# Seven block products for three column groups of a Fourier mixing layer, with fewer stored sums, on one NeuronCore

## The chip, the cores and the metric

One core of a Trainium2 chip. The metric is the time of one execution in microseconds of the device, lower is better. Engines are called by their short names: PE (TensorE, matmul), PEld (its weight loads), DVE (VectorE), ACT (ScalarE), POOL (GpSimd), SP (SyncE, which here issues most DMAs).

## What is computed

The input x has 2048 rows of 512 numbers. Four layers follow each other, each added to its input after a layer norm of the rows: transform, attention, transform, attention.

```python
x = x + A(layernorm(x)); x = x + B(layernorm(x)); x = x + A(layernorm(x)); x = x + B(layernorm(x))

def A(x):                       # Fourier mixing, real part
    a = x @ dft_hid_re.T; b = x @ dft_hid_im.T
    return dft_seq_re @ a - dft_seq_im @ b

def B(x):                       # 32 heads of 16, four segments of 512 rows
    q, k, v = heads(x @ wq), heads(x @ wk), heads(x @ wv)
    for each segment s:
        p = softmax(q_s k_s^T * scale + mask)       # mask as the reference has it
        o_s = g * (phi(q_s) M / (phi(q_s) z + 1e-6)) + (1 - g) * p v_s
        M += phi(k_s)^T v_s; z += sum(phi(k_s))
    return o @ wo
```

## The kernel before

The transform is taken in the order sequence first, hidden second. For a column group `tcn` of 512 output positions (four of them, `TC`), the kernel forms u = x^T C and x^T S over the 2048 rows, with C and S the 512 columns of the real and imaginary sequence matrix, and then multiplies by the hidden matrices (`hidden`, `hidden_last`). The 2048 rows are 16 tiles of 128; tile k and tile k + 8 (`HALF` is 8) are used together in step k. Each operand is split into a high and a low part in a reduced float32 (`split`: ACT writes the high part, the low part is a subtraction on DVE, or on POOL where asked), and a product is three matmuls, high x high, high x low, low x high (`matmul3`). All matmuls go through one helper, line 82 of the profile; all split copies have line 96, the subtractions line 98, or 94 where DVE does both.

**Transform one** (`direct` is true) works on the plain form. `read_pairs(tcn, k)` loads the four 128x512 blocks of a step (real and imaginary part for tile k and tile k + 8), splits them into the tiles chi and clo (three buffers each), makes four sums of them on DVE, and stores the sums in DRAM (`sums`, 1 MB a step). `contract(tcn)` then makes 8 steps of 2 x 2 x 4 products, 384 matmuls a group, into all eight PSUM banks, and copies the banks out, four on ACT and four on DVE (negated). During column group 0 the rows are also normalised: `normalise` loads two row tiles, makes moments on DVE, the inverse root on POOL, the scaled rows on DVE, the high part on ACT and the low part on POOL, for the tiles xa.

**Transform two** uses seven products for eight, as in fast 2x2 block multiplication: with the rows halved at tile 8 and the columns of x halved at 256, the products P1 to P7 of 256x512 outputs need sums of the blocks of the sequence matrix (those that transform one has stored) and sums of the rows. `read_block` loads one block or stored sum (256 KB) into one of eight places of a ring (`cring`) and splits it. `product` makes P1 and P7 together, then P2 and P4, for all four column groups; each is 8 steps of 2 x 3 matmuls into two banks, 48 in all. `add_rows` loads the rows again, normalises them and makes the row sums xb and xs on DVE. `chained` runs P6, P5, P3 through the same two banks and adds into the results between them. `TERMS` and `CHAIN` tell which result takes which product; results c stay in SBUF.

The order of all work is written by hand: `place(order, generator, slots)` puts each step of a generator into a numbered slot, and slots run in order; a slot in the transforms is about one unit of six matmuls. From that program order a planner with a cost model makes the static order of every engine; `pin` and `keep_in_program_order` hold some instructions to program order, `tc.issue_after` holds one behind another, and `tc.high_priority` moves some forward. `a1`, `b1`, `a2`, `b2` are the first slots of the four layers; transform one has 32 x 8 = 256 slots of products.

**Attention.** For four heads at a time (a unit): `natural_max` makes scores and their row maxima (DVE, line 653), `max_rows` transposes these maxima and puts them by a DMA of ACT's queue into the stacked operand, so that the next scores come out with the maximum subtracted. `softmax_values` makes those transposed scores in ten banks; each is clipped at zero on its diagonal blocks (ACT, line 718), exponentiated (ACT, line 719), masked on POOL (line 722) and multiplied with the values. `output` transposes and scales the result (DVE) and adds the memory part (POOL, line 826). At the very end, `outproj_split` prepares three quarters of each output row tile early, and `transpose_last` the last quarter, which waits for the last unit; then the last matmuls (po), an addition (line 170) and the store.

Of the kernel before, what the change touches and what calls it, by code (L numbers as in the profile page):

```python
# [18 lines left out]
P = 128  # L19
S, D, H = 2048, 512, 32  # L20
DH = D // H
# [20 lines left out]
SOURCE = {"P1": (0, 0), "P2": (0, 1), "P3": (1, 1), "P5": 0, "P7": 1, "P6": 2, "P4": 3}  # L42
# [4 lines left out]
    "P4": (((1, 0), (1, 1), ALU.add),),  # L47
}
CHAIN = {"P6": (1, 0), "P5": (1, 1), "P3": (0, 1)}
PHASES = (  # L50
    (("P1", "P7"), range(4)),
    (("P2", "P4"), range(4)),
)
# [3 lines left out]
def spectral_infini_kernel(  # L57
# [115 lines left out]
    v_tiles = [consts.tile([P, H, VW], F32, name=f"vt{i}") for i in range(6)]  # L173
# [12 lines left out]
    def run_from(t, n, step=1):  # L186
# [3 lines left out]
        (tcn, k): dram.tile([4, P, 512], F32, name=f"sum{tcn}_{k}") for tcn in range(TC) for k in range(HALF)  # L190
# [10 lines left out]
    def place_spectral(x_in, x_out, t0, end, ln_at, direct):  # L201
        xa, xb, xs, us, wdt, c, right = ({} for _ in range(7))
        start = t0
        count = [0]
        ring = []
# [57 lines left out]

        def new_right(src):
            tag = ("chi", "clo")[count[0] % 2]
            count[0] += 1
            t = pair(tag, tag, 3)
            split(t[:, 0], t[:, 1], src)
            return t

        def read_block(tcn, name, k):
            if not ring:
                ring.append(sb.tile([P, 2 * LT, 512], F32, name="cring", tag="xT", bufs=1))
            raw = ring[0][:, blocks_read[0] % (2 * LT)]
            blocks_read[0] += 1
            j = SOURCE[name]
            with tc.issue_after(last_stack[0].ins):
                if isinstance(j, tuple):
                    nc.sync.dma_start(raw, ct[j[0], tcn, k, :, j[1]])
                else:  # L280
                    nc.sync.dma_start(raw, sums[tcn, k][j])
            yield
            right[tcn, name, k] = new_right(raw)
            yield

        blocks_read = [0]

        def read_pairs(tcn, k):
            if not ring:
                ring.append(sb.tile([P, 8, 512], F32, name="sring", tag="xT", bufs=1))  # L290
            if k % 2 == 0:
                raw = [pair("craw", "craw", 2, F32) for _ in range(2)]
            else:
                raw = [ring[0][:, 0:2], ring[0][:, 2:4]]
            halves = [slice(0, 1), slice(1, 2)] if (tcn, k) == (0, 0) else [slice(0, 2)]
            for h in halves:
                for cc in range(2):
                    nc.sync.dma_start(raw[cc][:, h], ct[cc, tcn, k, :, h])
            yield
            for cc in range(2):  # L300
                right[tcn, cc, k] = pair("chi", "chi", 3), pair("clo", "clo", 3)
            for h in halves:
                for cc in range(2):
                    hi, lo = right[tcn, cc, k]
                    with behind_first((tcn, k) == (0, 0)):
                        split(hi[:, h], lo[:, h], raw[cc][:, h])
            yield
            t = ring[0][:, 4:]
            (r0, r1), (i0, i1) = ([raw[cc][:, h] for h in range(2)] for cc in range(2))
            for j, p, q in (0, r0, i0), (1, i0, i1), (2, t[:, 0], i1), (3, t[:, 2], r1):  # L310
                with behind_first((tcn, k) == (0, 0)):
                    summed = pin(V.tensor_tensor(out=t[:, j], in0=p, in1=q, op=ALU.add))
            if (tcn, k) == (1, 0):
                later.append(summed)
            nc.sync.dma_start(sums[tcn, k].rearrange("j p s -> p j s"), t)
            yield
# [5 lines left out]
        def contract(tcn):  # L322
            ps = [[bank(f"u{d}") for d in range(DT)] for _ in range(2)]
            for k in range(HALF):
                for h2 in range(2):
                    for cc in range(2):
                        parts = right[tcn, cc, k]
                        for d in range(DT):
                            matmul3(
                                ps[cc][d],  # L330
                                lambda h: xa[k + HALF * h2][:, h, d * P : (d + 1) * P],
                                lambda h: parts[h][:, h2],
                                (k, h2) == (0, 0),
                                (k, h2) == (HALF - 1, 1),
                            )
# [12 lines left out]

        def product(tcn, name):
            ps = [bank(f"m{m}") for m in range(2)]  # L350
            for k in range(HALF):
                t = right[tcn, name, k]
                for m in range(2):
                    matmul3(
                        ps[m],
                        lambda h: left(name, k, h, m),
                        lambda h: t[:, h],
                        k == 0,
                        k == HALF - 1,
                    )  # L360
                if k < HALF - 1:
                    yield
            for j, base, _ in TERMS[name]:
                if base != j:
                    block(tcn, j)
            for m in range(2):
                for j, base, op in TERMS[name]:
                    dst = c[tcn, j][:, m]
                    if base is None:
                        A.activation(dst, ps[m], AF.Copy)  # L370
                    else:
                        V.tensor_tensor(out=dst, in0=c[tcn, base][:, m], in1=ps[m], op=op)
            yield

        def chained(tcn):
            ps = [bank(f"m{m}") for m in range(2)]
            for name, j in CHAIN.items():
                for k in range(HALF):
                    t = right[tcn, name, k]
                    for m in range(2):  # L380
# [3 lines left out]
                            lambda h: t[:, h],  # L384
# [67 lines left out]
        for n, t in ln_at:  # L452
            place(3, normalise(n), [t, t, t] if n[0] == 0 and direct else [t - 8, t - 3, t])
        if direct:
            for tcn in range(TC):
                t = start + 8 * HALF * tcn
                place(2, contract(tcn), run_from(t, 4 * HALF, 2))
                for k in range(HALF):
                    place(3, read_pairs(tcn, k), [t + 8 * k - 12, t + 8 * k - 4, t + 8 * k + 3])
        else:  # L460
            t = start
            for names, tcns in PHASES:
                for tcn in tcns:
                    for n, name in enumerate(names):
                        at = run_from(t + n, HALF, len(names))
                        place(2, product(tcn, name), at)
                    for k in range(HALF):
                        for n, name in enumerate(names):
                            u = t + k * len(names) + n
                            place(3, read_block(tcn, name, k), [u - 10, u - 4])  # L470
                    t += HALF * len(names)
            u = t
            for tcns in (0, 1), (2, 3):
                at = {tcn: [] for tcn in tcns}
                for name, tcn in itertools.product(CHAIN, tcns):
                    at[tcn] += run_from(t, HALF)
                    for k in range(HALF):
                        place(3, read_block(tcn, name, k), [t + k - 10, t + k - 4])
# [3 lines left out]
            for k in range(HALF):  # L482
                place(3, add_rows(k), [u - 48 + 6 * k, u - 44 + 6 * k])
# [17 lines left out]
    def place_attention(x_in, x_out, t0, w_at, out_at):  # L501
# [195 lines left out]
        def softmax_values(s, g, u):  # L697
# [4 lines left out]
            def scores(dst, *cols):  # L702
# [15 lines left out]
                A.activation(blocks, blocks, AF.Relu)  # L718
# [80 lines left out]
        def output(s, g, u):  # L799
# [15 lines left out]
            for j in range(0, LT, 2):  # L815
# [5 lines left out]
                if s > 0:  # L821
# [4 lines left out]
                    G.tensor_tensor(out=dst, in0=dst, in1=tmp, op=ALU.add)  # L826
# [101 lines left out]
        def transpose_last(s):  # L928
# [9 lines left out]
            split(t[:, 0], t[:, 1], pt)  # L938
# [62 lines left out]
        for n in range(NSEG * USEG):  # L1001
# [3 lines left out]
            place(1.9, max_rows(*unit(n)), [t - 4])  # L1005
            place(1, natural_max(*unit(n)), run_from(t - 17, 10), [t - 7])
            place(0.5, stack(*unit(n)), [t - 21])
        for s in range(NSEG):
# [12 lines left out]
            if s == NSEG - 1 and x_out is out_tiles:  # L1021
                for i in range(LT):
                    place(2, outproj_split(s, i), [o - 12 + i], range(o - 7 + 3 * i, o - 7 + 3 * i + 3), [o + 5 + 1, o + 7])
# [32 lines left out]
    b1 = a1 + TC * 8 * HALF + LEAD  # L1056
# [18 lines left out]
    def setup():  # L1075
        nonlocal ident, ident_b, mask, same_head, gate
        with tc.issue_after(later[0].ins):
# [17 lines left out]
            for v in v_tiles:  # L1095
                G.memset(v[:, :, DH:], 1.0)
# [10 lines left out]
    ident = ident_b = mask = same_head = gate = None  # L1107
    place(5, setup(), [200])
    for t in sorted(slots):
# [45 lines left out]
```

## Time and profile before

| | us |
|---|---|
| median of 3 runs | 1826.85 (1824.24 to 1829.63) |
| the profiled execution | 1832.06 |
| its span, first to last instruction | 1830.3 |
| PE, DVE, ACT, POOL busy | 1776.4, 1300.4, 1053.2, 522.7 |
| products of transform one, first to last start | 7.3 to 362.8 |
| products of transform two, first to last start | 919.0 to 1247.9 |

Groups of instructions are read as: line, engine, operation, output <- inputs with shapes, count, then busy time in us and mean duration of one in ns, then the idle time of the engine just before them and who ended it. A table by stretch gives busy us and, in brackets, the count of instructions begun in the stretch; behind them the granted clock of PE, the busy share of the DMA engines and GB/s. A timeline merges equal neighbours; a bracket behind a line is the idle time before it. Line 98 is every low part, whichever tile it writes; the tile's name tells them apart. Durations of neighbouring instructions of one engine overlap a little, so their sum exceeds its busy time.

### The profile page before, as it was taken

The numbers are of one execution on the slowest core, as the hardware profiler recorded it, in microseconds if no ns is written. First come the engines' busy times: TensorE is split into PE (matmuls) and PEld (weight loads), VectorE is DVE, ScalarE is ACT, GpSimd is POOL, SyncE is SP. The second block draws the span as 40 slices with busy tenths as digits, with TensorE's granted clock in tenths as the row PEclk, the third lists the DMA queues.
The fourth block names the chain that finished last, engine by engine and source line by source line (L and its number), as shares of the span: only waits on it lengthen the run. The fifth ranks groups of instructions, "written<-read, shape, count | busy, mean of one in ns | idle before, by whom it ended". The sixth has DMA issues, their size and how long they took to land. (4 is left out here: it accounts for less than half of the span.)

```text
span 1830.3 us, 31933 instructions
## 1 busy us (share of the span) xinstructions
PE 1776.4 (97%) x10336; PEld 1288.4 (70%) x10336; DVE 1300.4 (71%) x4004; ACT 1053.2 (58%) x2292; POOL 522.7 (29%) x822
## 2 busy tenths in 40 slices
PE   7999999999999999999999999999999999999998
PEld 6788888888656666665568888888875666666654
DVE  7854445574787887877966787667658778787784
ACT  3221222333588787778774555444428787877785
POOL 4400000003344354445531100000134443534442
PEclk9999999999999999999999999999999999999999
DMA  6766665555453443443556777664546334344341
GB/s 220 232 221 197 201 199 185 172 167 169 129 169 123 148 135 99 154 126 126 165 173 198 228 245 220 196 189 133 159 152 186 123 122 152 114 135 141 106 128 42
DMA packets 165656, 296.50 MB, mean 162 GB/s; under 512 B 17776, under 2 KB 66928, under 8 KB 165488
## 3 DMA queue, kind: packets, MB, share of 16 engines
q1 hardware_dynamic: 162224, 293.68, 50.7%
q8 instruction: 81, 1.33, 0.3%
q10 hardware_dynamic: 3264, 0.79, 0.2%
q14 instruction: 87, 0.71, 0.1%
HBM read 192.95 MB, written 100.66 MB: 160 GB/s over the span
## 5 line engine op out<-in xcount | busy, mean ns | idle before, releaser
L653 DVE CUSTOM_DVE_ANT_0 junk<-nat,mask 128x512 bf16<-128x512 f32 (+3 forms) x1024 | 496.6, 485 | 160.7 <-PE nat L82 125.4
L719 ACT ACTIVATE pT<-sT 128x512 f32<-128x512 f32 x640 | 371.5, 598 | 13.1 <-ACT sT L718 0.7
L722 POOL TENSOR_SCALAR_AFFINE_SELECT pT<-pT 128x256 f32<-128x256 f32 (+1 forms) x448 | 197.3, 454 | 476.3 <-ACT pT L719 371.6
L82 PE MATMUL u<-chi,xa 128*128 128x512 f32 x1024 | 317.1, 391 | 7.3 <-DVE xa L94 7.3
L82 PE MATMUL sT<-stkq,stkk 99*128 99x256 bf16 (+3 forms) x1024 | 250.9, 307 | 5.4 <-DMA stkq<-mt 2.1
L82 PE MATMUL nat<-stkk,stkq 96*128 96x512 bf16 (+3 forms) x1024 | 246.7, 302 | 4.5 <-DVE mx L653 2.3
L718 ACT ACTIVATE sT<-sT 128x256 f32<-128x256 f32 (+1 forms) x640 | 208.8, 336 | 50.9 <-PE sT L82 48.2
L82 PEld LDWEIGHTS u<-chi,xa 128*128 128x128 f32 x1024 | 193.2, 189 | 47.1 <-issue 7.3
L145 POOL TENSOR_TENSOR r<-ve,half_neg 128x2 f32<-128x2 f32 (+2 forms) x24 | 19.7, 822 | 657.0 <-DVE ve L143 654.6
L82 PE MATMUL u<-clo,xa 128*128 128x512 f32 x512 | 201.6, 394 | 2.3 <-DVE clo L98 1.9
L82 PE MATMUL y<-wdt,us 128*128 128x512 f32 x768 | 181.9, 390 | 0.0
L82 PEld LDWEIGHTS <-stkk 99*128 99x128 bf16 x1024 | 82.2, 99 | 133.8 <-issue 119.5
L82 PEld LDWEIGHTS y<-wdt,us 128*128 128x128 f32 x768 | 143.6, 188 | 29.7
L82 PE MATMUL pv_bank<-pT,vt 128*17 128x512 f32 (+3 forms) x2048 | 151.6, 436 | 0.0
L82 PEld LDWEIGHTS <-stkq 96*128 96x128 bf16 x1024 | 94.8, 99 | 58.6 <-issue 17.3
L82 PE MATMUL pvv<-wv,xT 128*128 128x512 f32 x384 | 127.3, 443 | 3.6 <-DVE mx L653 3.6
L82 PE MATMUL pqk<-xT,wq 128*128 128x512 f32 x384 | 129.9, 448 | 0.1
L82 PE MATMUL po<-wo,oh 128*128 128x512 f32 x384 | 125.0, 441 | 3.7 <-DVE mx L653 2.2
L82 PE MATMUL pqk<-xT,wk 128*128 128x512 f32 x384 | 123.5, 430 | 0.0
L82 PEld LDWEIGHTS u<-clo,xa 128*128 128x128 f32 x512 | 96.5, 189 | 27.2 <-DVE clo L98 7.4
L82 PEld LDWEIGHTS pv_bank<-pT,vt 128*17 128x17 f32 x2048 | 54.1, 97 | 85.8 <-issue 82.3
L96 ACT ACTIVATE chi<-cring 128x512 fp32r<-128x512 f32 x112 | 70.6, 631 | 64.0 <-DVE clo L98 32.8
(136 smaller groups left out, 3015.9 us busy)
## 6 DMA issues: line engine op xcount, KB each, us to landing
sum<-sring SPq DMA_DIRECT2D x32, 1024.0 KB
cring<-sum SPq DMA_DIRECT2D x128, 256.0 KB
stkq<-scrq SPq DMA_DIRECT2D x64, 384.0 KB
stkk<-scrk SPq DMA_DIRECT2D x64, 384.0 KB
cring<-in_ct SPq DMA_DIRECT2D x96, 256.0 KB
sring<-in_ct SPq DMA_DIRECT2D x32, 512.0 KB
xt<-mid SPq DMA_DIRECT2D x64, 256.0 KB
craw<-in_ct SPq DMA_DIRECT2D x30, 512.0 KB
```

The source lines that it names most:

```text
L82: return tc.keep_in_program_order(op(*args, **kwargs))
L96: pin(A.activation(hi, src, AF.Copy, scale=scale))
L145: G.tensor_tensor(out=r, in0=ve, in1=half_neg[:, :n], op=ALU.pow)
L653: last_max[0] = V.tensor_tensor_reduce(junk[:, :n], src, mask[:, 512 - n :], 1.0, 3e38, ALU.add, ALU.min, dst,)
L718: A.activation(blocks, blocks, AF.Relu)
L719: A.activation(dst, ps, AF.Exp, scale=-SCALE)
L722: G.affine_select(blocks, blocks, pattern=[[0, n] for n in blocks.shape[1:-1]] + [[1, P]], compare_op=ALU.is_ge, fill=0.0, base=0, channel ...
```

## The change

Transform one: column group 0 stays in the plain form (`read_plain`, `contract`), with three of its sums on DVE and one on POOL, made in place in the loaded blocks. When a step's rows have been used, `change_rows` joins the high and low part again on POOL (`whole`), subtracts one half of the columns from the other (POOL) and splits that half anew (`replace`). Column groups 1 to 3 take seven products: P1, P2, P7, P4 step by step together (`read_all`), for the three groups one after the other; then `join_rows` makes the row sums out of the same tiles, on POOL and DVE, and P6, P5, P3 follow together for the three groups (`read_rest`). For these groups one sum is stored with the first pass (index 1), and one with the second (index 0), where four were stored. The loads land in a set of places of two blocks each: four in the ring, two in craw and three in the memory of the value tiles `v_all`, whose ones are set later (`ones`). The stores of sums go through ACT's queue. The sequence matrices lie in DRAM with the four blocks of a step side by side.

Transform two: P1 comes with P7 and P2 with P4 as pairs (`read_pair`); for groups 1 to 3 the second of the pair is made on POOL out of P1's or P2's block and the stored sum. P6, P5, P3 are read for two steps at once (`read_two`).

End of attention two: in the last three units the clips at zero of the odd heads go to DVE; the last unit's memory addition goes from POOL to DVE; the last quarter's split is made in two halves; the last unit's `max_rows` comes a slot earlier; the last row tile's matmuls are placed later.

The diff, cut to its core:

```diff
+    "P6": tuple((j, j, ALU.subtract) for j in ((1, 0), (1, 1), (0, 1))),
+    "P5": tuple((j, j, ALU.add) for j in ((1, 1), (0, 1))),
+    "P3": (((0, 1), (0, 1), ALU.add),),
...
+BLOCK = {"P2": 0, "P1": 1, "P3": 3}
+SUMMED = {"P5": (1, 0), "P7": (2, None), "P6": (3, 1), "P4": (0, None)}
...
+        def whole(i):
+            xn = sb.tile([P, D], F32, name="xn", bufs=2)
+            hi, lo = (xa[i][:, h].bitcast(F32) for h in range(2))
+            G.tensor_tensor(out=xn, in0=hi, in1=lo, op=ALU.add)
+            return xn
+        def replace(i, part, src):
+            split(xa[i][:, 0, part], xa[i][:, 1, part], src, lo_engine=G)
+        def change_rows(k):
+            xn = whole(k)
+            G.tensor_tensor(out=xn[:, b], in0=xn[:, a], in1=xn[:, b], op=ALU.subtract)
+            replace(k, b, xn[:, b])
+        def join_rows(k):
+            e, o = whole(k), whole(k + HALF)
+            V.tensor_tensor(out=e[:, b], in0=e[:, b], in1=o[:, b], op=ALU.add)
+            V.tensor_tensor(out=e[:, a], in0=e[:, b], in1=e[:, a], op=ALU.subtract)
+            V.tensor_tensor(out=o[:, a], in0=e[:, b], in1=o[:, a], op=ALU.subtract)
+            replace(k, a, e[:, b]); replace(k, b, e[:, a]); replace(k + HALF, a, o[:, a])
...
+        def read_plain(tcn, k):     # loads and splits as before, then, in place:
+                pin(V.tensor_tensor(out=re[:, 1], in0=re[:, 1], in1=im[:, 0], op=ALU.add))
+                pin(G.tensor_tensor(out=im[:, 0], in0=im[:, 0], in1=im[:, 1], op=ALU.add))
+                pin(V.tensor_tensor(out=im[:, 1], in0=re[:, 1], in1=im[:, 1], op=ALU.add))
+                pin(V.tensor_tensor(out=re[:, 0], in0=re[:, 0], in1=im[:, 1], op=ALU.add))
+            nc.scalar.dma_start(sums[tcn, k][:, :2], re)
+            nc.scalar.dma_start(sums[tcn, k][:, 2:], im)
+        def read_all(tcn, k):
+            fetch(re, ct[tcn, k, :, :2]); fetch(im, ct[tcn, k, :, 2:])
+            pin(G.tensor_tensor(out=im[:, 0], in0=im[:, 0], in1=im[:, 1], op=ALU.add))
+            later.append(pin(V.tensor_tensor(out=im[:, 1], in0=re[:, 1], in1=im[:, 0], op=ALU.add)))
+            right[tcn, "P2", k], right[tcn, "P1", k] = rights(re)
+            pin(V.tensor_tensor(out=re[:, 0], in0=re[:, 0], in1=im[:, 1], op=ALU.add))
+            split(hi[:, 0], lo[:, 0], im[:, 0]); split(hi[:, 1], lo[:, 1], re[:, 0])
+            nc.scalar.dma_start(sums[tcn, k][:, 1], im[:, 1])
+        def read_rest(tcn, k):      # two steps; x: P5 and P6 of one step, y: P3 of both
+                    pin(V.tensor_tensor(out=x[h][:, 0], in0=x[h][:, 1], in1=y[:, h], op=ALU.subtract))
+            right[tcn, "P5", k], right[tcn, "P6", k] = rights(x[0])
+            right[tcn, "P3", k], right[tcn, "P3", k + 1] = rights(y)
+            right[tcn, "P5", k + 1], right[tcn, "P6", k + 1] = rights(x[1])
+                    nc.scalar.dma_start(sums[tcn, k + h][:, 0], x[h][:, 0])
+        def read_pair(tcn, k, names):
+            fetch(two[:, 0], ct[tcn, k, :, BLOCK[names[0]]])
+            fetch(two[:, 1], summed(tcn, k, names[1] if tcn == 0 else "P6"))
+            if tcn:
+                op = ALU.subtract if names[1] == "P7" else ALU.add
+                pin(G.tensor_tensor(out=two[:, 1], in0=two[:, 1], in1=two[:, 0], op=op))
...
         if direct:
+            place(2, contract(0), run_from(t, 4 * HALF, 2))
+                place(3, read_plain(0, k), [t + 8 * k + d for d in (-12, -4, 1, 4)])
+                place(3, change_rows(k), [t + 8 * k + 9])
+            t += 8 * HALF
+            for tcn in range(1, TC):
+                for n, name in enumerate(names):            # P1, P2, P7, P4
+                    place(2, product(tcn, name), run_from(t + n, HALF, 4))
+                    place(3, read_all(tcn, k), [t + 4 * k + d for d in (-14, -7, -4, -2, 0)])
+                t += 4 * HALF
+                place(3, join_rows(k), [t + 6 * k - 28])
+            for tcn in range(1, TC):
+                for n, name in enumerate(CHAIN):            # P6, P5, P3
+                    place(2, product(tcn, name), run_from(t + n, HALF, 3))
+                    place(3, read_rest(tcn, k), [t + 3 * k + d for d in (-12, -6, -3, 0)])
+                t += 3 * HALF
...
-                A.activation(blocks, blocks, AF.Relu)
+                if x_out is out_tiles and (s * NG + g) * NU + u >= NSEG * USEG - 3 and cols[0][0] % 2:
+                    V.tensor_scalar_max(blocks, blocks, 0.0)
+                else:
+                    A.activation(blocks, blocks, AF.Relu)
...
-                    G.tensor_tensor(out=dst, in0=dst, in1=tmp, op=ALU.add)
+                    (V if last else G).tensor_tensor(out=dst, in0=dst, in1=tmp, op=ALU.add)
...
-            split(t[:, 0], t[:, 1], pt)
+            for half in slice(0, 2 * P), slice(2 * P, 4 * P):
+                split(t[:, 0, half], t[:, 1, half], pt[:, half])
...
-    b1 = a1 + TC * 8 * HALF + LEAD
+    b1 = a1 + (8 + 7 * (TC - 1)) * HALF + LEAD
```

More of the change, by code (lines that the diff above doesn't have):

```diff
@@ L203, in place_spectral @@
         start = t0
-        count = [0]
-        ring = []
+        homes, released, clock, singles = [], {}, [0], [0]
         def normalise(n):
@@ L262, in left, with raw_pair @@
             return src[:, h, (col + m) * P : (col + m + 1) * P]
-        def new_right(src):
-            tag = ("chi", "clo")[count[0] % 2]
-            count[0] += 1
+        def raw_pair(own=False):
+            clock[0] += 1
+            if not homes:
+                ring = sb.tile([P, 2 * LT, 512], F32, name="cring", tag="xT", bufs=1)
+                homes.extend(ring[:, j : j + 2] for j in range(0, 2 * LT, 2))
+                if direct:
+                    homes.extend(pair("craw", "craw", 2, F32) for _ in range(2))
+                    homes.extend(spare[:, j : j + 2] for j in range(0, 6, 2))
+            elif not direct and len(homes) == LT and clock[0] > 24:
+                homes.extend(pair("craw", "craw", 2, F32) for _ in range(2))
+            j = min((j for j in range(LT if own else len(homes)) if released.get(j, 0) is not None), key=lambda j: released.get(j, 0))
+            released[j] = None
+            return homes[j], j
@@ L286, in place_spectral @@
[L286 to L298, printed above, removed]
-            yield
[L300 to L306, printed above, removed]
-            yield
[L308 to L315, printed above, removed]
```

183 lines of the change are left out of this document (133 added, 50 removed).

## The prediction

> **What bounds the kernel now.** I read the page first, then the busy time of each engine by stretch, then who waits for whom on TensorE, then the groups by shape inside chosen stretches, and last the timelines of VectorE and GpSimd where both are busy.
>
> ```profile
> span 1830.3 us, 31933 instructions
> PE 1776.4 (97%) x10336; PEld 1288.4 (70%) x10336; DVE 1300.4 (71%) x4004; ACT 1053.2 (58%) x2292; POOL 522.7 (29%) x822
> ...
> L82 PE MATMUL u<-chi,xa 128*128 128x512 f32 x1024 | 317.1, 391 | 7.3 <-DVE xa L94 7.3
> L82 PE MATMUL u<-clo,xa 128*128 128x512 f32 x512 | 201.6, 394 | 2.3 <-DVE clo L98 1.9
> ```
>
> TensorE is busy for 97% of the span, and transform one is 1024 + 512 = 1536 of its matmuls. The mean of 391 ns is not what one costs, because matmuls overlap in the pipe; the cost is the spacing, and the table by stretch has it (busy us and count of each engine, then granted clock, DMA share, GB/s):
>
> ```profile
> core 0: us, PE busy (x) PEld busy (x) DVE busy (x) ACT busy (x) POOL busy (x), PEclk, DMA share, GB/s
> 31.40:42.76 11.36, 11.28 (x50) 8.85 (x49) 10.24 (x18) 2.97 (x5) 5.59 (x4) 1.00 0.74 233
> 186.00:272.00 86.00, 86.00 (x381) 71.19 (x381) 40.90 (x52) 18.41 (x19) 0.00 (x0) 1.00 0.59 193
> 965.00:1030.00 65.00, 64.76 (x293) 53.23 (x292) 44.99 (x79) 29.13 (x51) 11.77 (x10) 1.00 0.63 200
> 1054.00:1118.00 64.00, 64.00 (x284) 53.01 (x283) 57.42 (x110) 35.88 (x64) 0.00 (x0) 1.00 0.79 252
> ```
>
> In the second row (inside the third column group of transform one) 86.0 us hold 381 or 382 matmuls, 0.225 us each, with VectorE only 48% busy and GpSimd empty. So this stage is bound by TensorE alone, and a matmul less is 0.225 us less as long as that stays so. The last row is transform two, already in the seven-product form: 284 matmuls in 64 us, the same 0.225, although VectorE is at 90%. The first row is one of the eight steps of column group 0. A step is 48 matmuls, 10.8 us of TensorE, but it takes 11.36 us; the timeline of GpSimd shows the period, and VectorE is busy for 10.24 of it:
>
> ```profile
> 30.42 4.90 POOL L98 TENSOR_TENSOR xa<-xn,xa 128x512 fp32r<-128x512 f32 x2 [2.12 <-ACT xa L96]
> 38.96 0.69 POOL L145 TENSOR_TENSOR r<-ve,half_neg 128x2 f32<-128x2 f32 x1 [3.65 <-DVE ve L143]
> 41.78 4.90 POOL L98 TENSOR_TENSOR xa<-xn,xa 128x512 fp32r<-128x512 f32 x2 [2.12 <-ACT xa L96]
> ```
>
> So column group 0 is bound by VectorE, not by TensorE. Why VectorE needs 10.24 us shows when its groups from 20 to 95 us (first three rows, GpSimd active) are set against the same groups from 120 to 340 us (last three, GpSimd empty):
>
> ```profile
> L98 DVE TENSOR_TENSOR clo<-sring,chi 128x1024 fp32r<-128x1024 f32 x8 | 13.5, 1685 | 0.4 <-ACT chi L96 0.2
> L312 DVE TENSOR_TENSOR sring<-sring 128x512 f32<-128x512 f32 x12 | 11.0, 957 | 0.0
> L312 DVE TENSOR_TENSOR sring<-sring,craw 128x512 f32<-128x512 f32 x8 | 9.8, 1229 | 0.0
> ...
> L312 DVE TENSOR_TENSOR sring<-sring 128x512 f32<-128x512 f32 x41 | 26.4, 685 | 2.9 <-DMA sum<-sring 2.9
> L98 DVE TENSOR_TENSOR clo<-sring,chi 128x1024 fp32r<-128x1024 f32 x20 | 24.5, 1223 | 53.3 <-ACT chi L96 53.3
> L312 DVE TENSOR_TENSOR sring<-sring,craw 128x512 f32<-128x512 f32 x20 | 13.7, 685 | 0.1
> ```
>
> The same subtraction takes 1685 instead of 1223 ns, the sums 957 and 1229 instead of 685. Per step that is 2 x 0.46 for the subtractions and about 4 x 0.29 for the sums (a mean over the two rows and the six sums that stayed at 0.69), 2.1 us beside two GpSimd subtractions. So one GpSimd 128x512 operation costs VectorE about 1.05 us here. What it takes GpSimd itself undisturbed, and what a narrow one takes, are in these two rows (timeline, then chain of waits):
>
> ```profile
> 448.62 1.17 POOL L593 TENSOR_TENSOR parts<-rem,parts 128x512 bf16<-128x512 f32 x1 [0.74 <-ACT parts L589]
> ...
> 1821.15 0.46 POOL onat L826
> ```
>
> 1.17 us for 512 columns, 0.46 for 128; I take 0.70 for 256, between them. In transform two the price is smaller. Groups from 965 to 1030 us, with three GpSimd pairs, and from 1054 to 1118 us, with none:
>
> ```profile
> L98 DVE TENSOR_TENSOR clo<-cring,clo 128x512 fp32r<-128x512 f32 x19 | 15.0, 792 | 5.1 <-ACT clo L96 5.1
> L98 DVE TENSOR_TENSOR chi<-cring,chi 128x512 fp32r<-128x512 f32 x19 | 14.5, 763 | 6.5 <-ACT chi L96 5.8 <-DMA xt<-mid 0.7
> L166 DVE TENSOR_SCALAR xn<-xt,row_mv,row_r 128x512 f32<-128x512 f32 x8 | 5.3, 699 | 0.1
> ...
> L98 DVE TENSOR_TENSOR clo<-cring,clo 128x512 fp32r<-128x512 f32 x24 | 16.5, 687 | 2.3 <-ACT clo L96 2.1
> L372 DVE TENSOR_TENSOR c<-c,m 128x512 f32<-128x512 f32 x11 | 7.3, 681 | 0.6 <-PE m L82 0.6
> L166 DVE TENSOR_SCALAR xn<-xt,row_mv,row_r 128x512 f32<-128x512 f32 x14 | 7.2, 542 | 0.0
> L241 DVE TENSOR_TENSOR xn<-xn 128x256 f32<-128x256 f32 x7 | 2.9, 419 | 0.0
> ```
>
> The excess is 19 x 0.105 + 19 x 0.076 + 8 x 0.157 = 4.7 us for six GpSimd operations, 0.78 each. The c<-c,m rows read PSUM, and two that ran beside a GpSimd pair kept their time:
>
> ```profile
> 1009.19 1.37 DVE L372 TENSOR_TENSOR c<-c,m 128x512 f32<-128x512 f32 x2 [1.76 <-PE m L82]
> ...
> 1009.63 3.00 POOL L98 TENSOR_TENSOR xa<-xn,xa 128x512 fp32r<-128x512 f32 x2 [4.19 <-ACT xa L96]
> ```
>
> So p, the loss of VectorE for one more GpSimd 128x512 operation, lies between 0 (beside idle time or such evictions) and 1.05 us. By width, a 256-column operation counts 0.6 p. The whole forecast hangs on p.
>
> The Trainium skill, page "SBUF — State Buffer", section "Who interferes with whom", says that a VectorE instruction with two SBUF inputs contends with a GpSimd instruction that reads SBUF, and that the one that comes second is blocked for the whole instruction of the other. The trace agrees with 1685 against 1223 ns, and with the unchanged PSUM evictions. By that rule alone, each new operation in a saturated queue would cost its 1.17 us, about the upper end; that is the second rival below.
>
> **The change part by part** (plus is slower).
>
> *Matmuls.* Column groups 1 to 3 go from 384 to 7 x 8 x 2 x 3 = 336 matmuls each: 3 x 48 x 0.225 = **-32.4 us**. Transform two keeps its 1344.
>
> *Column group 0 (bound by VectorE, 11.36 us a step).* VectorE loses one sum (-0.685). GpSimd gets one sum (1), the joining of the two halves (1), a 256-column subtraction and a 256-column remainder (0.6 each), 3.2 p a step. Ends: at p = 0 the step falls to TensorE's 10.8, -0.56; at 1.05 it is +2.68. Over seven steps -4 to +19. At p = 0.5 it is +0.92 a step: **+6**.
>
> *Products P1, P2, P7, P4 of groups 1 to 3.* A step is 24 matmuls, 5.4 us. VectorE: one subtraction of 1.22, two of 0.685, two sums of 0.685, and 6 evictions in 8 steps, together 4.47 us by durations. Durations overlap: in the stretch 1054:1118 the nine groups sum to 65.2 us and the engine was busy 57.42, so I scale by 0.88 to 3.93. With one GpSimd sum it is 3.93 + p, under 5.4 for every p: **0**. Three buffers of each of chi and clo leave four of the step's six-matmul units, 5.4 us, to refill one, against 1.22 us of VectorE and 1.06 of ScalarE:
>
> ```profile
> L96 ACT ACTIVATE chi<-sring 128x1024 fp32r<-128x1024 f32 x32 | 33.5, 1059 | 103.9 <-PE u L82 84.0 <-DVE sring L312 14.9 <-DMA sring<-in_ct 4.9
> ```
>
> DMA: 1 MB in and 0.25 MB out in 5.4 us is 243 GB/s, and the row 1054:1118 ran at 252 with TensorE unbroken: 0.
>
> *Joining the rows, eight times, in the 49 six-matmul units (66 us) before the last is needed.* GpSimd: two 128x512 and three 128x256, 3.8 p. VectorE: three of 0.42, scaled 1.1. All eight: 8 x (1.1 + 3.8 p). Room: 37.8 us at (3.93 + p)/5.4, then 28 us of the last three products, where two steps (8.1 us) need three subtractions of 1.22, two of 0.685 and three evictions, scaled 6.25 (77%). At p = 0.5: 24 us to place, 6.8 + 6.4 us of room: **+11**. Ends: 0 at p = 0; 40.8 - 9.4 = +31 at 1.05. What is queued behind a late remainder is the first use of these rows as P6, P5 and P3, that is TensorE itself.
>
> *Handing over banks.* After P6, P5 and P3 of a group VectorE makes 12 evictions, 8.2 us by 0.681, while TensorE finds two spare banks and reaches P6's banks after 4.05 us. Ends 0 and 3 x 4.2 = +12.5; it has the two other products to run through, so I stay near the low end: **+2**.
>
> *Queues.* The sums' writes move from SP to ScalarE's queue, 16 + 24 + 24 issues. The nearest row is a 0.73 us issue during which ScalarE went on working:
>
> ```profile
> 1800.74 0.58 ACT L719 ACTIVATE pT<-sT 128x512 f32<-128x512 f32 x1
> 1800.99 0.73 ACTq L692 DMA_DIRECT2D stkq<-mt  x1
> 1801.22 0.27 ACT L718 ACTIVATE sT<-sT 128x128 f32<-128x128 f32 x1
> ```
>
> Even if each blocked it, a step of 5.4 us would have about 2 x 1.06 + 0.73 of ScalarE: 0. SP no longer holds loads behind a store, but TensorE lost nothing to loads: 0. The ones in the value tiles are set later, 0.9 us of GpSimd beside other work: 0.
>
> *Transform two.* 48 GpSimd additions between load and split. In 1054:1118 (23.7 steps of 12 matmuls) VectorE has 6.6 us free and needs 23.7 p more: +5 at p = 0.5, 0 to +18 over its ends. In 965:1030 it is 45.0 + 24 p in 65 us: 0 (to +5). **+5**.
>
> *End of attention two.* The waits of TensorE, the chain of waits, and the clips' group from 1797 us on:
>
> ```profile
> PE sT L82 <- ACT pT L719: 1.5, 1, 1.5
> PE oT L82 <- POOL onat L826: 0.8, 1, 0.8
> PE po L82 <- ACT oh L96: 0.7, 1, 0.7
> ...
> 1821.15 0.46 POOL onat L826
> 1821.65 0.86 PE oT L82 x4
> 1822.54 0.60 ACT oh L96
> ...
> L718 ACT ACTIVATE sT<-sT 128x256 f32<-128x256 f32 (+1 forms) x18 | 5.6, 327 | 0.0
> ```
>
> Four of ten clips at zero per unit leave ScalarE (0.33 us each), which takes most of the 1.5 us stall; VectorE's addition in place of 0.46 saves some 0.2, half a copy before the first use 0.25. Ends -4 (all three waits and a little more) and +1 (clips queue behind maxima): **-2**.
>
> *Sum:* -32.4 + 6 + 0 + 11 + 2 + 0 + 5 - 2 = -10.4 us. The profiled execution took 1832.06 us (span 1830.3), so it would take 1821.7; it stands 5.2 us above the median of the runs, so the median goes from 1826.85 to **1816.5**. 0.3% (5.5 us) is about what a measurement of this kernel can tell from no change.
>
> **The rivals.**
>
> *Covered (p up to 0.25).* The planner puts the new GpSimd work beside evictions and waits. For it: VectorE at 48% before. Against: the joins leave no such place. At 0.25: -32.4 + 1 + 1.5 + 2 + 0 - 2 = -30, 1797.
>
> *Blocked (p about 0.78, transform two's own price).* VectorE and GpSimd take turns, and VectorE becomes the bound of transform one. -32.4 + 7 x 1.81 + (32.5 - 11.3) + 3 + 12 - 2 = +14.5, **1841**, slower. For it: both measured prices, 0.78 and 1.05. Against: those were pairs right behind a full VectorE queue. It decides from p = 0.62, where the sum is zero; at 1.05 it is over +40.
>
> *The matmuls go, the time does not: bank turn-around.* With p = 0.5 and the handover at its upper end of 12.5 us, the sum is 0, 1827. For it: the four interleaved products fill all eight banks. Against: each product ends six matmuls after the one before it, which staggers the evictions.
>
> **How the numbers follow.** Forecast (p from 0.35 to 0.55, 1804 to 1821) 0.33, covered 0.19, blocked 0.33, turn-around 0.15. Faster 0.33 + 0.19 = 0.52, same 0.15, slower 0.33. I take p = 0.5 because one end is measured where everything was queued and the other is what idle time gives; the new work meets both. Between 0.25 and 0.35, and above 0.55, the cases meet. The range runs from p about 0.25 to about 0.85: 1797 to 1846, with about 1 in 10 left out on either side; the likeliest case's own is 1804 to 1821.
>
> **What would show it.** Transform one has 1392 matmuls; in its groups 1 to 3 a count near 222 in 50 us with short gaps means covered, VectorE above 95% busy with subtractions above 1.4 us means blocked. A step of group 0 should last 12.3 us. A break should stand where the joins run, just after group 3's P4, and little at the handovers. In transform two the stretch with the row sums should lose about 5 us. I am wrong if TensorE waits on DMA in the new products, or if the shared memory of value tiles and loads delays the start of attention one.

## The result and the profile after

The change made the kernel slower: a median of 1857.08 us (1855.27 to 1859.52) against 1826.89, a ratio of 1.0163 with a 95% interval of 1.0151 to 1.0176. The forecast was 1816.5, with a range of 1797 to 1846; the rival "blocked" had 1841 and the right sign. In later comparisons the kernel before stood at 1831 to 1833 us, so each version below is compared with the runs of before beside it: the changed kernel is "30.2 above". Single runs of the kernel before went from 1827 to 1836 us there, so a version that ran once is read by its trace.

The page of the changed kernel, then the first and last starts of the hidden products (y) and of the first products with row sums in transform two (xb):

```profile
span 1857.8 us, 32230 instructions
PE 1761.4 (95%) x10192; PEld 1261.1 (68%) x10192; DVE 1455.6 (78%) x4113; ACT 1100.1 (59%) x2367; POOL 726.5 (39%) x964
...
L82 PE MATMUL y<-wdt,us x768: 387/389/501, 375.7 to 1387.2; 128*128 128x512 f32 x192
L82 PE MATMUL m<-chi,xb x192: 389/389/389, 1150.8 to 1258.0; 128*128 128x512 f32 x192
```

The 144 matmuls are gone (10336 to 10192), VectorE is busy 155 us longer and GpSimd 204. Set side by side, by first starts in the two traces:

| stretch of the traces | before | after | difference |
|---|---|---|---|
| first product to the 384th (column group 0) | 7.3 to 101.7 | 7.3 to 111.6 | +10 |
| from there to the first y | 261.4 | 264.1 | +2.7, with 32.4 us of matmuls less |
| first y to the first product of transform two | 555.9 | 556.7 | +1 |
| from there to the first xb product | 199.9 | 218.4 | +18.5 |
| from there to the last y | 236.5 | 236.4 | 0 |
| from there to the end | 474.9 | 470.6 | -4 |

So groups 1 to 3 of transform one gave back 35 us where 32.4 were won, and transform two lost 18.5 without a matmul changed. GpSimd's timeline in column group 0, one step long:

```profile
33.16 3.16 POOL L98 TENSOR_TENSOR xa<-xn,xa 128x512 fp32r<-128x512 f32 x2 [1.94 <-ACT xa L96]
36.28 2.27 POOL L256 TENSOR_TENSOR xn<-xa 128x512 f32<-128x512 f32 x1
38.64 1.60 POOL L265 TENSOR_TENSOR xn<-xn 128x256 f32<-128x256 f32 x1
40.77 0.73 POOL L98 TENSOR_TENSOR xa<-xn,xa 128x256 fp32r<-128x256 f32 x1 [0.53 <-ACT xa L96]
41.60 1.07 POOL L145 TENSOR_TENSOR r<-ve,half_neg 128x2 f32<-128x2 f32 x1
42.64 1.29 POOL L362 TENSOR_TENSOR craw<-craw 128x512 f32<-128x512 f32 x1
45.88 3.15 POOL L98 TENSOR_TENSOR xa<-xn,xa 128x512 fp32r<-128x512 f32 x2 [1.94 <-ACT xa L96]
```

The step is 12.7 us where it was 11.36. The joining addition (line 256) takes 2.27 us, the sum of the same size (line 362) 1.29. In the same step on VectorE:

```profile
35.10 4.54 DVE L98 TENSOR_TENSOR clo<-craw,chi 128x1024 fp32r<-128x1024 f32 x2
42.71 1.24 DVE L150 TENSOR_TENSOR rt<-r 128x2 f32<-128x2 f32 x1 [0.59 <-POOL r L145]
```

The two wide subtractions and the joining addition lie over each other from 36.28 us on. Line 150 begins 0.07 us behind GpSimd's sum and ends with it, at 43.95 against 43.93 us. VectorE's groups in that part (20 to 107 us), then between 230 and 300 us, where the rows are joined, then in transform two from 1086 to 1150 us:

```profile
L98 DVE TENSOR_TENSOR clo<-cring,chi 128x1024 fp32r<-128x1024 f32 x6 | 13.7, 2300 | 0.0
L150 DVE TENSOR_TENSOR rt<-r 128x2 f32<-128x2 f32 x6 | 7.4, 1239 | 3.6 <-POOL r L145 3.6
...
L98 DVE TENSOR_TENSOR clo<-cring,chi 128x1024 fp32r<-128x1024 f32 x8 | 13.2, 1660 | 0.0
...
L166 DVE TENSOR_SCALAR xn<-xt,row_mv,row_r 128x512 f32<-128x512 f32 x14 | 13.1, 962 | 0.0
```

The wide subtraction takes 2300 ns, against 1685 before and 1223 alone; the row scaling 962 against 542. Line 150 works on two numbers a partition and takes 1.24 us; before it took 0.16:

```profile
L150 DVE TENSOR_TENSOR rt<-r 128x2 f32<-128x2 f32 x7 | 1.1, 162 | 6.1 <-POOL r L145 6.1
```

The table by stretch, transform one where the rows are joined, then transform two:

```profile
200.00:250.00 50.00, 45.83 (x194) 35.38 (x192) 47.15 (x49) 20.43 (x33) 31.19 (x21) 1.00 0.53 173
250.00:300.00 50.00, 41.55 (x165) 31.02 (x164) 46.12 (x50) 21.54 (x33) 31.87 (x24) 0.97 0.45 155
...
1000.00:1050.00 50.00, 46.84 (x195) 36.68 (x193) 38.38 (x54) 19.38 (x34) 29.01 (x20) 0.97 0.62 202
1050.00:1100.00 50.00, 49.64 (x218) 40.77 (x219) 44.63 (x59) 25.64 (x44) 21.15 (x14) 1.00 0.68 220
1100.00:1150.00 50.00, 45.39 (x188) 35.77 (x187) 49.93 (x81) 23.91 (x44) 18.29 (x10) 0.97 0.67 217
```

222 matmuls would be a full stretch. VectorE is at 92 to 100% in the rows that lose most but one: from 1000 to 1050 us it is at 77%, and 27 matmuls are missing all the same. The granted clock of 0.97 in three of the rows is a stretch of 3.4 us at half clock in each: matmuls stand 0.43 us apart in it, 8 in place of 15, so it can cost 1.6 us. Transform two has three such stretches (before, its products had none), but they do not make its loss: a version below, without the early row changes, has one there and takes 219.0 us, not less than 218.4. In the row from 1000 to 1050 us GpSimd's queue had just stood still for 12.9 us, with additions behind a remainder that waited for ScalarE:

```profile
986.02 1.28 POOL L422 TENSOR_TENSOR cring<-cring 128x512 f32<-128x512 f32 x1
1000.22 3.00 POOL L98 TENSOR_TENSOR xa<-xn,xa 128x512 fp32r<-128x512 f32 x2 [12.93 <-ACT xa L96]
1003.18 2.99 POOL L422 TENSOR_TENSOR craw<-craw 128x512 f32<-128x512 f32 x2
```

That gave two theories. "Port": GpSimd and VectorE take turns and lengthen each other's instructions. "Queue": the new work stands behind operations that wait, in an engine that executes in order.

### The profile page after: what moved, and what is told of

It is laid out like the page before. It is cut to its first block, busy times and chain, and to the rows that moved or that the text cites. A ratio compares the mean times of both kernels' runs of the same rounds, so it can differ in the third digit from the quotient of the medians.

```text
span 1857.8 us, 32230 instructions
## 1 busy us (share of the span) xinstructions
PE 1761.4 (95%) x10192; PEld 1261.1 (68%) x10192; DVE 1455.6 (78%) x4113; ACT 1100.1 (59%) x2367; POOL 726.5 (39%) x964
## 3 DMA queue, kind: packets, MB, share of 16 engines
q8 instruction: 80, 1.31, 0.3%
## 4 chain that ended last, share of the span: by engine, by line
PE 66%; DVE 17%; issue 6%; POOL 5%; DMA 3%; ACT 2%; SPq 0%; DVEq 0%; ACTq 0%; POOLq 0%
PE m L82 16%; PE pqk L82 9%; PE y L82 8%; PE pv_bank L82 7%; PE sT L82 7%; PE nat L82 6%; PE pvv L82 4%; PE po L82 3%; DVE junk L787 3%; DVE clo L98 3%; POOL xa L98 2%; DVE c L495 2%; PE on L82 1%; PE pm L82 1%; DVE xn L166 1%
## 5 line engine op out<-in xcount | busy, mean ns | idle before, releaser
L82 PE MATMUL m<-chi,xa 128*128 128x512 f32 x1056 | 316.9, 400 | 11.1 <-ACT chi L96 3.1
L82 PE MATMUL m<-clo,xa 128*128 128x512 f32 x720 | 238.0, 401 | 18.6 <-DVE clo L98 18.4
L82 PEld LDWEIGHTS m<-chi,xa 128*128 128x128 f32 x1056 | 201.7, 192 | 58.9 <-DVE c L495 4.3
L82 PEld LDWEIGHTS m<-clo,xa 128*128 128x128 f32 x720 | 135.9, 190 | 59.4 <-DVE clo L98 32.5
L96 ACT ACTIVATE chi<-cring 128x512 fp32r<-128x512 f32 (+1 forms) x137 | 99.5, 730 | 110.3 <-PE m L82 46.7
L82 PE MATMUL pv_bank<-pT,v_all 128*17 128x128 f32 (+3 forms) x2048 | 153.7, 436 | 1.3 <-POOL pT L859 1.3
L82 PEld LDWEIGHTS pv_bank<-pT,v_all 128*17 128x17 f32 x2048 | 53.6, 97 | 89.5 <-issue 84.3
```

Of the source, the lines that this page charges most:

```text
L82: return tc.keep_in_program_order(op(*args, **kwargs))
L96: pin(A.activation(hi, src, AF.Copy, scale=scale))
```

## The experiments

**All new work on VectorE.** The additions, remainders and differences that the change gave to GpSimd run on VectorE.

```diff
-                pin(G.tensor_tensor(out=two[:, 1], in0=two[:, 1], in1=two[:, 0], op=op))
+                pin(V.tensor_tensor(out=two[:, 1], in0=two[:, 1], in1=two[:, 0], op=op))
...
-            split(xa[i][:, 0, part], xa[i][:, 1, part], src, lo_engine=G)
+            split(xa[i][:, 0, part], xa[i][:, 1, part], src)
```

> All additions and remainders that the change gave to GpSimd run on VectorE. Theory 'port': a GpSimd operation costs a busy VectorE about what its own would (0.6 to 1.05 us against 0.6), so little moves: 1842 to 1857 us, a step of column group 0 stays at 12.7 us (11.36 + 0.61 + 2 x 0.36 for the three operations). Theory 'queue': GpSimd executes in order, and its work for the matmuls stands behind operations that wait (12.9 us at 987 us, 10.7 at 205); then the losses of transform two (18.5 us) and of the joins mostly go: 1825 to 1838, with group 0 unchanged.

Measured: 1826.64 us against 1832.82, ratio 0.9967 (0.9955 to 0.9978). The number lies in the range of "queue", but that range was set from 1826.9 us for the kernel before, so it meant 2 us faster to 11 slower, and 6 faster lies outside it. The wording of "queue" fails too: the step of group 0 fell from 12.7 to 11.6 us, which it had as unchanged. The first y starts at 347.1 (375.7 with GpSimd), and transform two takes 207.2 us (218.4). In the step only the old GpSimd remainders are left; the joining addition still meets them:

```profile
34.50 1.76 DVE L256 TENSOR_TENSOR xn<-xa 128x512 f32<-128x512 f32 x1 [1.19 <-POOL xa L98]
...
L98 DVE TENSOR_TENSOR clo<-cring,chi 128x1024 fp32r<-128x1024 f32 x6 | 7.3, 1217 | 0.0
```

The subtractions are back at 1217 ns. "A GpSimd operation costs VectorE what its own would" was too cheap: taking over the work made VectorE's other work shorter. It is busy 1426.0 us here, with all of the new work, and 1455.6 in the changed kernel, where GpSimd does part of it. The version is 6 us below before where the changed kernel is 30 above.

**The kernel before, with the rows' low parts on VectorE.**

```diff
-                engines = ... else {"lo_engine": G, "hi_engine": A}
+                engines = ... else {"lo_engine": V if direct else G, "hi_engine": A}
```

> The kernel before, with the low parts of the normalised rows of transform one on VectorE in place of GpSimd. Port: the two subtractions cost VectorE 2.1 us a step on GpSimd and 1.2 on its own queue, so the step falls from 11.36 to TensorE's 10.8: 3 to 4 us faster, 1823. Rival (offloading does relieve VectorE): its step grows by 1.2 us, 8 us slower, 1835.

Measured: 1833.10 against 1832.82, ratio 1.0 (0.9987 to 1.0012). Both expectations miss. From 20 to 100 us, first this kernel, then the kernel before:

```profile
20.00:100.00 80.00, 77.69 (x338) 62.95 (x337) 65.80 (x127) 24.61 (x32) 4.18 (x6) 1.00 0.71 230
...
20.00:100.00 80.00, 79.57 (x340) 62.44 (x339) 70.14 (x111) 23.47 (x31) 37.53 (x20) 1.00 0.71 229
```

VectorE was relieved by 4.3 us, as "port" says, and TensorE made no more matmuls (338 and 340). So column group 0 of the kernel before was not held by VectorE's load. What holds its step at 11.36 us instead of 10.8 stays open.

**Transform two: GpSimd writes a constant instead of adding.** Same place in the queue, same wait for the load of the block that is written, nothing read (the sums for P7 and P4 of groups 1 to 3 are left out). **And: subtractions of the same size, on memory that nothing waits for.** They wait for no load either.

```diff
-                pin(G.tensor_tensor(out=two[:, 1], in0=two[:, 1], in1=two[:, 0], op=op))
+                pin(G.memset(two[:, 1], 0.001))
...
+                v5 = v_tiles[5][:, :, :DH]
+                pin(G.tensor_tensor(out=v5, in0=v5, in1=v5, op=ALU.subtract))
```

> The 48 additions of transform two are replaced by a GpSimd write of a constant into the same block, at the same place in its queue and with the same waits (left out: the sums for P7 and P4 of three column groups). It reads nothing. Port: all 18.5 us of transform two come back, about 1838. Queue: the first stretch (970 to 1056 us, some 10 us) stays lost, only the stretch with the row sums (some 8) comes back: 1847 to 1850.

> The 48 additions are replaced by GpSimd subtractions of the same size on memory that nothing waits for (left out: the same sums). They read, but no split waits for them. Port: the loss stays, 1852 to 1857. Queue: the first stretch comes back (10 us), the row sums' stretch stays: 1845 to 1849.

Measured: 1844.14 us and 1854.13, 11 and 21 above before. Transform two to its first xb product took 201.6 us with writes and 210.6 with the operations apart, against 199.9 before and 218.4 in the changed kernel. First the writes, then the operations apart:

```profile
1000.00:1050.00 50.00, 48.78 (x216) 40.04 (x215) 35.50 (x65) 23.55 (x41) 12.17 (x17) 1.00 0.71 223
1050.00:1100.00 50.00, 50.00 (x222) 41.40 (x221) 38.88 (x69) 26.26 (x46) 9.10 (x17) 1.00 0.75 231
...
L422 POOL MEMSET cring<- 128x512 f32 x34 | 18.1, 536 | 45.7 <-DMA cring<-sum 45.7
...
1000.00:1050.00 50.00, 46.50 (x195) 36.98 (x194) 38.37 (x53) 19.51 (x34) 27.45 (x23) 0.97 0.64 196
1050.00:1100.00 50.00, 46.86 (x199) 35.74 (x199) 49.30 (x62) 24.47 (x43) 26.32 (x20) 1.00 0.67 213
```

With writes, 17 of the 18.5 us are back, though they stand in the same queue behind the same remainders (longest wait there 14.3 us). "Queue" had the first stretch as lost; it is not, so a waiting queue head alone does not cost this time. With reading operations that nobody waits for, 10.7 us stay lost and 7.8 come back. "Port" had all of it staying and "queue" about 8 us, with the first stretch restored, which it is not (195 matmuls). So contention by itself is the larger part, and the rest appears when the splits also wait for the slowed additions. Each of the two ran once, but this stretch repeats: the changed kernel and the next two versions, which leave it as it is, took 218.4 to 219.0 us. One difference stays: a write takes 0.54 us and an addition 1.3 to 1.7, so the chain was shorter too. With the additions done on VectorE (the first experiment) the stretch took 207.2 us. The Trainium skill, page "SBUF — State Buffer", section "Who interferes with whom", has VectorE's two-input instructions contend with GpSimd's reads and not with its writes; 201.6 against 218.4 us agrees.

**Transform one without the early row changes, and without the joins.** The two `place` lines of `change_rows` and of `join_rows` are taken out, one in each kernel.

> The changed kernel without change_rows (left out: the subtraction of one half of the columns from the other in the eight early row tiles, so P7, P5 and P6 read the plain rows). Port: the GpSimd operations of a step fall from 6 to 3 and the step of column group 0 from 12.7 to about 11.2 us, so group 0 ends near 100 us in place of 111; all else stays: about 11 us less than the changed kernel, 1846. Rival (group 0 is held by the moved sum and the in-place order): it stays near 111, 1857.

> The changed kernel without join_rows (left out: the row sums for P6, P5 and P3). Port and queue both: the matmuls missing between 232 and 300 us come back, some 18 us, 1839. Rival (the bank handovers of P6, P5 and P3 lose the time): no more than 5 us come back, 1852.

Measured: 1855.85 and 1838.64 us, 24 and 7 above before (the changed kernel is 30 above). Without the changes the step is 11.56 us and the 384th matmul starts at 104.5, nearer to the 100 of "port" than to its rival's 111, although line 150 still takes 1.24 us. The first y comes 10.8 us earlier, at 364.9, of which 3.7 are left at the end of the trace; the rest is lost in stretches that this version does not touch, 2.9 between the first y and transform two and 3.7 behind the last y. Without the joins the first y comes at 351.4, 24.3 earlier:

```profile
250.00:300.00 50.00, 48.09 (x211) 39.01 (x210) 37.46 (x46) 17.76 (x17) 0.00 (x0) 1.00 0.57 189
```

211 matmuls where the changed kernel has 165. The joins are the larger part, and the bank handovers alone are not what was lost. But this version leaves out the joins' work on VectorE and ScalarE too, so the 24.3 us are not GpSimd's alone.

**The kernel before with the new end alone.**

> The kernel before with nothing but the new end of attention two. From the two traces: the distance from the last row-maximum matmul's stage to the end is 4.3 us shorter, so 4 us faster than before. The prediction's own term: 2 us.

Measured: 1831.98 against 1831.47, ratio 1.0 (0.999 to 1.0009). The end brings nothing that the runs can tell (the interval is about 1.8 us either way); in the traces the time from the last row-maximum matmul to the end fell from 33.0 to 32.1 us. The 4 us that the changed kernel seemed to win behind its last y are not from this edit: the stretch from the last y to the last row-maximum matmul, which no kernel here edits but for its last units, takes 441.9 us before, 438.5 changed, 442.0 here.

**All on VectorE, and the low parts too.** To the all-VectorE version come the low parts of transform one's rows on VectorE and an earlier start of transform two's row sums.

```diff
...
-                place(3, add_rows(k), [t - 48 + 6 * k, t - 44 + 6 * k])
+                place(3, add_rows(k), [t - 76 + min(12 * k, 28 + 6 * k), t - 72 + min(12 * k, 28 + 6 * k)])
```

> The version with all new work on VectorE, and further the low parts of transform one's rows on VectorE (no GpSimd reads left in column group 0) and the row sums of transform two begun earlier, at unequal distances from slot 56 on. Port: the step of group 0 goes from 11.6 to about 11, 4 us; transform two loses 2 to 4 us in place of 7: 8 us faster than the all-VectorE version, 0.8% faster than before. Rival (VectorE's own load is the bound now): no gain over the all-VectorE version, 0.3% faster than before.

Measured: 1821.92 against 1831.47, ratio 0.9947 (0.9932 to 0.9962). The first y starts at 343.6, 3.5 us earlier than in the all-VectorE version; transform two still takes 206.7 us where 3 to 5 us less were expected, and the gap moved to 1002 to 1018 us. The gain over before, 0.5%, lies between the two expectations (0.8 and 0.3%).

**That version with one kind of work back on GpSimd.** First the 32 sums, then the joining and changing of rows.

> The best version with only the sums of transform one (8 + 24) back on GpSimd; the joining of rows stays on VectorE. In the best version the hidden products of layer one start at 343.6 us, in the changed kernel at 375.7. Port: VectorE loses about what it is spared, so they start at 342 to 347. Queue (sums stuck behind joining work that waits): nothing waits in front of the sums here, so likewise 342 to 346; the two theories part on the next run.

> The best version with only the joining and splitting of rows (change_rows, join_rows) on GpSimd, the sums on VectorE. Port: the loss adds up, so most of the 32 us is here, hidden products start at 362 to 372 us, and the wide subtractions of VectorE in column group 0 take over 1.7 us. Queue: the loss needs both kinds on one queue; here at most 12 us, 346 to 356.

Measured: 1836.88 and 1829.21 us, against 1831.5 before. The first y starts at 356.9 and 352.1, 13.3 and 8.5 later than in the version without GpSimd. Both theories miss on the sums (342 to 347 expected); on the joins "port" misses (362 to 372) and "queue" is right (346 to 356). Together they are 21.8 us of the 32.1 between that version and the changed kernel; the rest needs both, or the low parts (3.5). Half of the sums' price has its place in group 0: its 384th matmul starts at 108.2 in place of 101.3, with VectorE's wide subtraction undisturbed and line 150 not:

```profile
L98 DVE TENSOR_TENSOR clo<-cring,chi 128x1024 fp32r<-128x1024 f32 x6 | 7.3, 1221 | 0.0
...
L150 DVE TENSOR_TENSOR rt<-r 128x2 f32<-128x2 f32 x6 | 7.4, 1238 | 5.3 <-POOL r L145 5.3
```

One GpSimd sum a step falls on the first of the small operations between the moments and the scaled rows, and adds 1.08 us to the chain that the next step's rows wait for; the step is 12.0 us. In the version without that sum line 150 takes 154 ns. The other 6.4 us are lost behind group 0, and where is not shown. With the joining and changing of rows on GpSimd the 384th matmul starts at 100.5: alone, the row changes cost nothing in group 0, while taking them out of the changed kernel brought 7.1 us there. So the losses do not add.

**The row sums ten slots later.** `t - 66 + min(10 * k, 18 + 6 * k)` for the first of the two slots.

> The best version with the row sums of transform two begun 10 slots later and evenly spaced, so that they do not meet the last normalised rows (1002 to 1018 us, some 4 us of matmuls missing there). If that meeting makes the gap: 2 to 4 us faster than the best version, 0.7% faster than before. If ScalarE's wait for the normalised rows makes it (5.4 us idle at 1001 us): no change, 0.5% faster.

Measured: 1819.48 against 1831.52, ratio 0.9934 (0.9913 to 0.9954), the best of all; its interval overlaps that of the version before it. Transform two takes 203.9 us to its first xb product, 2.8 less, which is what the first reading gave (2 to 4). From 1000 to 1050 us 15 matmuls are still missing, so ScalarE's wait remains a candidate for the rest:

```profile
1000.00:1050.00 50.00, 47.33 (x207) 38.31 (x206) 44.52 (x84) 26.16 (x46) 3.66 (x3) 1.00 0.72 234
```

## Why the prediction was wrong

- *Matmuls, -32.4 us:* right. 144 are gone at 0.225 us each, and in the best version, with the work and the low parts on VectorE, 19.9 us of it arrive (first y at 343.2 against 363.1).
- *Column group 0, +6:* measured +10. Worked back, a step of +1.34 us is p = 0.63, not 0.5. The reading that VectorE's load holds this part was wrong (relieving it by 4.3 us changed nothing); in the changed kernel the wide subtractions took 2.30 us and the operation of 0.16 us became 1.24. Neither is the whole of it: without the row changes the 1.24 stay and the step is 11.56. With the row changes on GpSimd and nothing else of it, group 0 loses nothing either. What makes the step 12.7 us when they come together is not separated.
- *Joins +11 and handover +2:* measured 35. This is the term that was mis-sized most: leaving the joins out brings 24.3 us back, and leaving the new work and the low parts off GpSimd in all of transform one, group 0 with it, 32.1. With all of it on VectorE the stretch behind group 0 still takes 242.3 us, 13 more than 261.4 less 32.4: as much as the two terms gave. So about 22 of the 35 us go with the engine.
- *Products P1, P2, P7, P4, 0:* nearly so where the joins do not run: 216 of 222 matmuls from 150 to 200 us.
- *Transform two, +5:* measured +18.5. Only the stretch with the row sums was given a loss; the stretch before it, priced at 0 by VectorE's average load, lost as much. An average over 65 us does not see a wait between a load, an addition and a split.
- *End, -2:* -0.9 in the traces, nothing that the runs can tell.
- *Queues and DMA, 0:* not contradicted; without GpSimd 220 of 222 matmuls ran from 150 to 200 us in the first of the two best versions.
- *The step that failed* is the choice p = 0.5 for the price of a GpSimd operation. It took 0, the price beside idle time, as one end of equal weight. Both prices that the trace had measured, 0.78 and 1.05, stood on the other side of the break-even point at 0.62 that the prediction itself gave. The traces differ by 27.5 us; p = 0.78 gives 14.5, and 1.05 over 40. Worked back stage by stage with the prediction's own terms, p is 0.63 in group 0, about 1.1 at the joins (35 with 2 for the handover) and 1.06 in transform two. So the upper price has two of the three terms in size, and for transform two that is partly luck: half of its loss stood in the stretch where the term was 0. A price per operation counts VectorE's time, and leaves out that GpSimd's joining addition is lengthened as well (2.27 us; the shortest 1.27) and that the matmuls wait for it. How much this makes is argued, not shown. Two signs that the prediction named for "blocked" and for the joins did come: subtractions above 1.4 us (2.30 in group 0) and a break at the joins (165 matmuls from 250 to 300 us).

What share of the losses in transform one is contention as such, and what share in-order waiting behind a slowed operation, is not separated: no run there kept the waits and took only the reads away.

## What to carry to other kernels

Before work is given to GpSimd, look whether VectorE is busy there with instructions that take two operands from SBUF: if a trace shows one pair of operations that lengthened each other, take that price for every new one, not a mean with zero; here the two prices measured before stood for 14.5 and over 40 us, around the 27.5 that came, and the mean forecast a gain. Keeping the work on VectorE can be the better choice: here, with VectorE busy 71% of the span before, the same change was 1.6% slower with GpSimd and 0.3% faster without it, 0.7% with two further moves. A tiny operation in a serial chain can lose as much to a collision as a wide one.

## What the runs showed of the hardware

GpSimd's additions and VectorE's instructions on the same stretch of time waited for each other. In column group 0 of the changed kernel 0.16 us became 1.24 for 2 columns a partition and 1.22 became 2.30 for 1024, both 1.08 more. The small one began 0.07 us behind a GpSimd sum of 1.29 us and ended with it: what it lost is what was left of that sum, and not a share of its own length. The price is not fixed: with only the joining and changing of rows on GpSimd, eleven of sixteen wide subtractions in that part kept 1.22 us and the others took 1.31 to 2.31. GpSimd's joining addition became 2.27 us, the shortest took 1.27. The row scaling, which has only one wide input, was lengthened too, from 0.54 to 1.5 us in seven of fourteen cases from 1086 to 1150 us, each beside a GpSimd addition. GpSimd writes of the same shape (0.54 us) left TensorE at 216 and 222 matmuls in stretches where reading operations left 195 and 199.
